# Moving the copies and the short transform of the middle column in a Fourier mixing and feed-forward kernel

## The chip, the cores and the metric

The kernel runs on one core of a Trainium2 chip. The metric is the device time of one execution in microseconds (us). The kernel before took 1976.9 us as the median of three runs (1976.07 to 1977.3). The profiled execution took 1976.83 us, of which 1975.0 us lie between its first and last instruction (the span).

## The reference

The input x has 8 batches of 3008 rows and 256 columns. Each batch is transformed along both axes and the real part kept; then every row goes through a feed-forward layer with the activation h cos(h).

```python
X = np.fft.fft(x, axis=1)
X = np.fft.fft(X, axis=2)
x = X.real.astype(np.float32).reshape(B * S, D)      # 24064 x 256
h = x @ w_in                                         # 256 -> 2048
g = h * np.cos(h)
out = g @ w_out                                      # 2048 -> 256
```

All types are float32.

## The kernel before

**The transform.** The 3008 rows are split as 47 x 64. A first half transforms over the 47 (`first_half`, eight chunks of a batch, two chunks for each quarter of x), its result goes to DRAM (`store_z`) and comes back in another layout (`load_z`), and a second half transforms over the 64 (`second_half`, six groups). The transform over the 256 columns is folded into the weights of the feed-forward layer. Since x is real, columns d and 256 - d are folded into their sum and difference (`fold`). Column 128 has no partner; it is called the middle column here. It is taken by itself: `take_middle` (L287) copies column 128 of one quarter of x, 94 x 8 numbers, on ScalarE into `xm`; `middle` (L291) clears 64 x 32 numbers of a PSUM bank on VectorE, adds two short matmul calls (four records in the profile) and copies the sum to `zm` on ScalarE. `keep_z` (L276), which takes each chunk out of PSUM, copies four columns of `zm` into it.

**The loop.** The feed-forward layer of a batch runs in 48 steps (six groups of columns by eight pieces of the 2048), 384 steps in all. The loop at L832 goes by half steps: `k` counts them, `t` is the step and `u` its half (0 even, 1 odd). While batch b goes through its 48 steps, batch b + 1 is transformed piece by piece: `transform` (L376) puts its calls into a list by step, and they are issued at the end of the odd half of that step (L909). For a quarter p of x, the load stands in step 2p, its copy of the middle column in step 2p + 2, the folds in steps 8p + 6 to 8p + 10, and a pair of first-half chunks in the even half of step 8p + 12. `middle` stands in step 10. "Step 10 of batch 1" below is the step 10 during which batch 1 is in the feed-forward layer and batch 2 is transformed. In batch 7 nothing is left to transform. Batch 0 follows an opening, in which batch 0 is transformed and the weights are loaded and folded; some of this is spread over steps 0 to 22 of batch 0 (`opening`, L797: sums of `w2` on POOL, and second halves in steps 5, 10, 14, 18 and 22).

**A half step.** The program writes every engine's instructions in an order fixed by hand, and each engine runs its own in that order. For half k (called cur; prev is k - 1, old is k - 2) the order is: `mm1(cur, 0)` on PE (L514) and `act_e` on ACT (L526, writes `ew`); in the even half of a step with a pair, the first chunk; `dve_g(old)` on DVE (L556) and, in every other half, `sums` on POOL (L572 to L579); the second chunk of a pair; `mm2` on PE (L605, three matmul calls of an older step); `act_round(prev)` on ACT (L542); the seed of half k + 1 on ACT (L495, which writes PSUM for the next `mm1`); `dve_frac(prev)` on DVE (L546); `act_sin(prev)` on ACT (L552); `mm1(cur, 1)` on PE; in some halves one more call of `mm2`; and `dve_h(cur)` on DVE (L530).

**Banks.** Four PSUM banks are handed out in turn to the halves (`psum` with tag H). `borrow(name, k)` takes the bank whose turn comes after k more, without taking the turn; its last user must be through with it.

**Transfers.** SP issues all of the loads and nearly all of the stores, in the order of the program. In the table of DMA traffic the opening fills the DMA engines for its first 70 us.

Of the kernel before, what the change touches and what calls it, by code (L numbers as in the profile page):

```python
# [22 lines left out]
NI = 32  # L23
# [85 lines left out]
def kernel(  # L109
# [7 lines left out]
    nc = tc.nc  # L117
# [85 lines left out]
    def psum(name, tag="H"):  # L203
        at = tag
        if tag == "H":
            at = f"H{turn[0] % 4}"
            turn[0] += 1
        return ppool.tile([128, 512], FP, tag=at, bufs=bank[tag], name=name)

    def borrow(name, k=0):  # L210
        return ppool.tile([128, 512], FP, tag=f"H{(turn[0] + k) % 4}", bufs=1, name=name)
# [28 lines left out]
    def first_half(b, c, pz=None):  # L240

        rows = 2 * N2 if b else 128
        fv = xfs.pop((b, c)).rearrange("r (e c) -> r e c", e=2)[0:rows]
        LE, LO, LE0, LO0 = (L[0:rows, 64 * q : 64 * q + 64] for q in range(4))
        pz = pz or psum("pz", "M")
        a = 128 if c == 0 else 0
        for e, (w, w0) in enumerate(((LE, LE0), (LO, LO0))):
            rows = slice(64 * e, 64 * e + 64)
            if a:
                nc.tensor.matmul(  # L250
                    pz[rows, 0:128], lhsT=w0, rhs=fv[:, e, 0:128], start=True, stop=True
                )
            nc.tensor.matmul(  # L253
                pz[rows, a:512],
                lhsT=w,
                rhs=fv[:, e, a:512],
                start=not a,
                stop=True,
                skip_group_check=True,
            )  # L260
        if b:
            return pz
        if a:
            nc.tensor.matmul(
                pz[64:128, 0:1], lhsT=LE0, rhs=fv[:, 1, 0:1], start=True, stop=True
            )
        nc.tensor.matmul(
            pz[64:128, a:512:128],
            lhsT=LE,
            rhs=fv[:, 1, a:512:128],  # L270
            start=True,
            stop=True,
        )
        keep_z(b, c, pz)

    def keep_z(b, c, pz):  # L276
        tag, n = ("zs", 4) if b or c < 4 else ("pq", 8)
        zs = spool.tile([128, 512], FP, tag=tag, bufs=n, name="zs")
        nc.scalar.copy(out=zs, in_=pz)
        if b:  # L280
            nc.scalar.copy(out=zs[64:128, 0:512:128], in_=zm[64:128, IP * c : IP * c + IP])
        zss[b, c] = zs

    xm = cpool.tile([128, NI], FP, tag="xm", name="xm")
    zm = cpool.tile([128, NI], FP, tag="zm", name="zm")
# [2 lines left out]
        xv = xs[b, p].rearrange("r (i d) -> r i d", d=ND)[0 : 2 * N2]  # L288
        nc.scalar.copy(out=xm[0 : 2 * N2, XP * p : XP * p + XP], in_=xv[:, :, 128])

    def middle(b):  # L291
        pm = borrow("pm")[64:128, 0:NI]
        nc.vector.memset(pm, 0.0)
        for i0, i1, q in ((0, 1, 2), (1, NI, 0)):
            nc.tensor.matmul(
                pm[:, i0:i1],
                lhsT=L[0 : 2 * N2, 64 * q : 64 * q + 64],
                rhs=xm[0 : 2 * N2, i0:i1],
                start=False,
                stop=True,  # L300
                skip_group_check=True,
            )
        nc.scalar.copy(out=zm[64:128], in_=pm)

    zds = {}
    z2s = {}
# [64 lines left out]
        nc.scalar.copy(out=nb[:, 0:T], in_=pn[:, 0:T])  # L371

    pairs = {}
    per = NG * 8

    def transform(b):  # L376
        todo = {}

        def at(o, *call):
            todo.setdefault(o, []).append(call)  # L380

        for p in range(4):
            at(2 * p, load_x, b, p)
            at(2 * p + 2, take_middle, b, p)
            for k in range(4):
                at(8 * p + (6, 7, 9, 10)[k], fold, b, 2 * p + k // 2, k % 2)
            pairs[per * (b - 1) + 8 * p + 12] = b, 2 * p
            for c in (2 * p, 2 * p + 1):
                at(8 * p + 12, store_z, b, c)
        at(10, middle, b)  # L390
        at(23, load_z, b, 0)
        at(39, load_z, b, 1)
        for g in range(NG):
            at(42 + g, second_half, b, g)
        return todo
# [138 lines left out]
    def sides(h):  # L534
        T = h.s.T
        return h.s.r[:, 2 * T * h.u : 2 * T * h.u + 2 * T], h.H[:, 0 : 2 * T]

    def act_round(h):
        if h.u == 0:
            h.s.r = spool.tile([128, 1024], FP, tag="r", bufs=4, name="r")  # L540
        r, y = sides(h)
        nc.scalar.activation(out=r, in_=y, func=AF.Copy, bias=BIG, scale=1.0)  # L542
# [41 lines left out]
    def mm2(s, lo, hi, order=range(7)):  # L584
        T = s.T
        key = (s.b, s.grp)
        if s.fp == 0 and lo == 0:
            acc[key] = []
            started[key] = set()
        gv, sv = blocks(s)  # L590
        todo = (
            (0, wv[:, 0, 0, s.fp], gv[:, 0, 0]),
            (1, wv[:, 1, 0, s.fp], gv[:, 1, 0]),
            (2, vx[:, 3, s.fp], gv[:, 1, 1]),
            (3, vx[:, 1, s.fp], sv[:, 0]),
            (4, vx[:, 0, s.fp], sv[:, 1]),
            (5, vx[:, 2, s.fp], sv[:, 2]),
            (6, wv[:, 1, 1, s.fp], sv[:, 3]),
        )
        for m, w, a in (todo[i] for i in order[lo:hi]):  # L600
            first = m // 2 not in started[key]
            if first:
                acc[key].append(psum("M", "M"))
            started[key].add(m // 2)
            nc.tensor.matmul(  # L605
                acc[key][m // 2][:, 256 * (m % 2) : 256 * (m % 2) + T],
                lhsT=w,
                rhs=a,
                start=first,
                stop=s.fp == 7,  # L610
                skip_group_check=True,
            )
# [210 lines left out]
    def unit(k):  # L823
        return halves[k] if 0 <= k < 2 * n else None
# [7 lines left out]
    for k in range(2 * n + LAG):  # L832
        t, u = divmod(k, 2)
        d, v = divmod(k - LAG, 2)
        cur, prev, old, nxt = unit(k), unit(k - 1), unit(k - 2), unit(k + 1)
        done = step(d)
        full = step(d if v else d - 1, True)
        if cur:
            if k % (2 * per) == 0:
                todo = transform(cur.s.b + 1) if cur.s.b + 1 < NB else {}  # L840
            if k not in range(3, AHEAD):
                mm1(cur, 0)
                if t == 0:
                    seed_first(cur)
                act_e(cur)
            if k == 0:
                spread_nb()
                fold_weights(1, 3)
            elif k == 1:
                pw = weights(0, 3)  # L850
            elif k == 2:
                pw = weight_row(3)
        pair = None if u else pairs.pop(t, None)
        if pair:
            b, c = pair
            pz = [first_half(b, c, borrow("pz"))]
        if old:
            dve_g(old)
            if old.u:
                sums(old.s)  # L860
        if pair:
            pz.append(first_half(b, c + 1, borrow("pz", 1)))
        if done:
            order = (0, 1, 5, 4, 3, 2, 6) if done is steps[-1] else range(7)
            mm2(done, 4 * v, 4 * v + 3, order)
        if full and full is not steps[-1]:
            take_m(full, 1 if v else 3, nc.vector)
        if nxt and 0 < k < AHEAD - 1:
            seed(nxt)
        if prev:  # L870
            act_round(prev)
        if pair:
            keep_z(b, c, pz[0])
        if nxt and k >= AHEAD - 1:
            seed(nxt)
        if full and full is not steps[-1]:
            take_m(full, 0 if v else 2, nc.scalar)
        if prev:
            dve_frac(prev)
        if k + 1 in range(3, AHEAD):  # L880
            mm1(nxt, 0)
            act_e(nxt)
        if prev:
            act_sin(prev)
        if pair:
            keep_z(b, c + 1, pz[1])
        if k == 1:
            keep_weights(0, 3, pw)
        elif k == 2:
            keep_wn(3, pw)  # L890
        if cur:
            mm1(cur, 1)
        if done and v == 0:
            mm2(done, 3, 4, order)
        if cur:
            dve_h(cur)
        if u == 0:
            continue
        for i in range(6):
            s = step(t - 4 - i, True)  # L900
            if s:
                combine_m(s, i)
        for sg, lag in ((0, 8), (1, 10)):
            s = step(t - lag, True)
            if s:
                store_out(s, sg)
        for call in opening.pop(t, ()):
            call[0](*call[1:])
        for call in todo.pop(t % per, ()):  # L909
            call[0](*call[1:])  # L910
# [31 lines left out]
```

## Time and profile before

| | |
|---|---|
| median of three runs | 1976.9 us |
| profiled execution | 1976.83 us |
| its span | 1975.0 us |
| busy: PE, ACT, DVE, POOL | 98%, 77%, 74%, 71% |
| granted TensorE clock, mean | 0.995 |

The span begins with the first instruction. PE is the matmul queue and PEld its weight loads; a row of the order of time has the start, the length, the engine, the line, what is written and read, and in brackets how long the engine stood idle before it and what ended that.

The length of a step can be read from the order of time: `act_e` (ACT, L526) runs once for each half, so the start of every second L526 marks a step, and the difference of two of them is a step's length. Some of these lengths, in us:

| step | batch 0 | batch 1 | batch 2 | batch 3 | batch 4 | batch 5 | batch 6 | batch 7 |
|---|---|---|---|---|---|---|---|---|
| 2 | 15.97 | 4.94 | 5.86 | 4.89 | 5.40 | 5.28 | 4.69 | 4.60 |
| 3 | 6.81 | 4.14 | 4.14 | 4.14 | 4.14 | 4.14 | 4.14 | 4.14 |
| 4 | 4.19 | 4.19 | 4.19 | 4.18 | 4.19 | 4.19 | 4.19 | 4.19 |
| 5 | 5.18 | 4.19 | 4.19 | 4.19 | 4.19 | 4.19 | 4.19 | 4.19 |
| 7 | 4.24 | 4.24 | 4.24 | 4.24 | 4.24 | 4.24 | 4.24 | 4.24 |
| 8 | 4.39 | 4.39 | 4.39 | 4.39 | 4.39 | 4.39 | 4.39 | 4.39 |
| 9 | 4.42 | 4.42 | 4.42 | 4.41 | 4.41 | 4.41 | 4.41 | 4.41 |
| 10 | 7.03 | 5.93 | 5.93 | 5.93 | 5.93 | 5.92 | 5.93 | 4.85 |
| 11 | 4.69 | 4.75 | 4.75 | 4.75 | 4.75 | 4.75 | 4.75 | 4.60 |
| 12 | 6.82 | 6.82 | 6.83 | 6.83 | 6.82 | 6.83 | 6.83 | 4.75 |
| 14 | 5.69 | 4.75 | 4.75 | 4.75 | 4.75 | 4.75 | 4.75 | 4.75 |
| 18 | 5.79 | 5.00 | 4.99 | 5.00 | 5.00 | 4.99 | 5.00 | 4.90 |
| 20 | 6.81 | 6.81 | 6.81 | 6.81 | 6.81 | 6.81 | 6.81 | 4.75 |

Steps 12 and 20 of batches 0 to 6 have a pair of first-half chunks. Groups of 225 columns go over into groups of 256 during steps 8 to 10.

### The profile page before, as it was taken

Reading aid. Unit: us, or ns where it says so; the run is one execution under the profiler, and the core shown is the slowest. Engines: PE = TensorE matmul, PEld = TensorE weight load, DVE = VectorE, ACT = ScalarE, POOL = GpSimd, SP = SyncE. Lnnn points to the kernel's source line nnn. Section 1 sums busy time; section 2 is a strip of 40 time slices with the busy share of each in tenths; the row PEclk is TensorE's granted clock in tenths of the full one; section 3 lists DMA queues with packets and bytes.
Section 4 is the critical chain, followed back from the end, with each engine's and each line's share of the span. In section 5 each row is a group of like instructions: output and inputs, shape, how many; then the busy total and the mean of one; then the engine's idle time right before and its main releaser. Section 6 shows DMA issues by size and latency. Waiting matters only on the chain.

```text
span 1975.0 us, 29718 instructions
## 1 busy us (share of the span) xinstructions
PE 1944.0 (98%) x9262; PEld 1688.1 (85%) x9262; DVE 1455.9 (74%) x2529; ACT 1519.6 (77%) x3450; POOL 1398.4 (71%) x1593
## 2 busy tenths in 40 slices
PE   9799999999999999999999999999999999999998
PEld 4788889888988889888888888988889888898887
DVE  3577778777777777777777777777777777778786
ACT  3577778777777777877878777777877787778775
POOL 3577767777677775778667876677766777666775
PEclk9899999999999999999999999999999999999999
DMA  8512014020241112301132022411114111100001
GB/s 200 118 25 46 22 41 85 22 42 19 46 82 26 36 26 59 71 18 40 40 60 51 20 41 41 84 23 38 26 41 85 24 40 28 38 22 16 12 15 29
DMA packets 176690, 88.70 MB, mean 45 GB/s; under 512 B 103303, under 2 KB 173622, under 8 KB 174902
## 3 DMA queue, kind: packets, MB, share of 16 engines
q1 hardware_dynamic: 176374, 86.68, 21.4%
q8 instruction: 75, 1.23, 0.3%
q14 instruction: 81, 0.66, 0.1%
q10 hardware_dynamic: 160, 0.13, 0.0%
HBM read 49.50 MB, written 37.27 MB: 44 GB/s over the span
## 4 chain that ended last, share of the span: by engine, by line
PE 89%; DMA 4%; DVE 3%; ACT 2%; SPq 1%; issue 0%; POOL 0%; DVEq 0%; ACTq 0%; POOLq 0%
PE M L605 53%; PE H L514 31%; PE pz L253 3%; DMA xp<-in_x_dram 2%; PE pb L339 2%; DVE r L546 1%; DMA zd<-zs 1%; ACT r L552 1%; DVE r L556 1%; ACT r L542 1%; DMA w<-in_moe_w_out_dram 0%; ACT ew L526 0%; DVE mr L630 0%; DMA wr<-in_moe_w_in_dram 0%; DMA out_dram<-ob 0%
## 5 line engine op out<-in xcount | busy, mean ns | idle before, releaser
L572 POOL TENSOR_TENSOR S<-r 128x512 f32<-128x512 f32 (+1 forms) x383 | 475.5, 1242 | 470.4 <-DVE r L556 423.5
L546 DVE SCALAR_TENSOR_TENSOR r<-r,H 128x512 f32<-128x512 f32 (+1 forms) x768 | 518.5, 675 | 222.3 <-ACT r L542 197.6
L552 ACT ACTIVATE r<-r 128x512 f32<-128x512 f32 (+1 forms) x768 | 477.5, 622 | 258.8 <-DVE r L546 256.2
L605 PE MATMUL M<-S,VX 128*128 128x256 f32 (+1 forms) x2304 | 615.7, 376 | 0.0
L556 DVE SCALAR_TENSOR_TENSOR r<-H,r 128x512 f32<-128x512 f32 (+1 forms) x768 | 518.8, 676 | 129.6 <-ACT r L552 86.6
L605 PEld LDWEIGHTS M<-S,VX 128*128 128x128 f32 x2304 | 435.9, 190 | 71.5 <-issue 22.7
L514 PE MATMUL H<-pq,WS 128*128 128x256 f32 (+1 forms) x1536 | 451.7, 376 | 11.9 <-ACT ew L526 11.9
L514 PE MATMUL H<-pq,WC 128*128 128x256 f32 (+1 forms) x1536 | 456.0, 379 | 2.8 <-ACT H L495 2.1
L542 ACT ACTIVATE r<-H 128x512 f32<-128x512 f32 (+1 forms) x768 | 447.5, 583 | 0.0
L530 DVE TENSOR_TENSOR H<-ew,H 128x256 f32<-128x256 f32 (+1 forms) x768 | 324.6, 423 | 139.7 <-PE H L514 79.3
L605 PE MATMUL M<-r,w 128*128 128x256 f32 (+1 forms) x1536 | 388.6, 375 | 0.0
L526 ACT ACTIVATE ew<-H 128x256 f32<-128x256 f32 (+1 forms) x768 | 288.3, 375 | 103.4 <-PE H L514 97.9
L495 ACT ACTIVATE H<-nb,wn 128x256 f32<-128x256 f32 (+1 forms) x766 | 365.6, 477 | 1.4
L514 PEld LDWEIGHTS H<-pq,WS 128*128 128x128 f32 x1536 | 290.9, 190 | 46.5 <-ACT ew L526 14.1
L605 PEld LDWEIGHTS M<-r,w 128*128 128x128 f32 x1536 | 300.5, 197 | 27.9 <-ACT mr L628 1.0
L514 PEld LDWEIGHTS H<-pq,WC 128*128 128x128 f32 x1536 | 280.0, 190 | 47.4 <-ACT H L495 15.1
L578 POOL TENSOR_TENSOR S<-S,r 128x256 f32<-128x256 f32 (+1 forms) x383 | 276.0, 721 | 30.0
L579 POOL TENSOR_TENSOR S<-r,S 128x256 f32<-128x256 f32 (+1 forms) x383 | 275.0, 718 | 30.0
L605 PE MATMUL M<-r,VX 128*128 128x256 f32 (+1 forms) x768 | 225.6, 375 | 0.0
L605 PE MATMUL M<-S,w 128*128 128x256 f32 (+1 forms) x768 | 225.2, 375 | 0.0
L605 PEld LDWEIGHTS M<-S,w 128*128 128x128 f32 x768 | 150.5, 196 | 14.6
L605 PEld LDWEIGHTS M<-r,VX 128*128 128x128 f32 x768 | 146.1, 190 | 14.7
(74 smaller groups left out, 927.4 us busy)
## 6 DMA issues: line engine op xcount, KB each, us to landing
out_dram<-ob SPq DMA_DIRECT2D x728, 32.0 KB
xp<-in_x_dram SPq DMA_DIRECT2D x56, 256.0 KB
zd<-zs SPq DMA_DIRECT2D x112, 96.0 KB
z<-zd SPq DMA_DIRECT2D x28, 384.0 KB
xp<-in_x_dram SPq DMA_DIRECT2D x56, 120.0 KB
nb<-nd SPq DMA_DIRECT2D x40, 128.0 KB
wr<-in_moe_w_in_dram SPq DMA_DIRECT2D x8, 256.0 KB
w<-in_moe_w_out_dram SPq DMA_DIRECT2D x4, 512.0 KB
```

The costliest lines, as they stand in the source:

```text
L495: nc.scalar.activation(out=h.H[:, 0:T], in_=s.nb[:, 0:T], func=AF.Copy, bias=0.25, scale=wn[:, f : f + 1])
L514: nc.tensor.matmul(h.H[:, 0:T], lhsT=W[:, 128 * f : 128 * f + 128], rhs=s.pq[:, e * T : e * T + T], start=False, stop=True, skip_group_che ...
L526: nc.scalar.mul(out=h.ew[:, 0:T], in_=h.H[:, 0:T], mul=2.0)
L530: nc.vector.tensor_tensor(out=h.H[:, T : 2 * T][:, ::-1], in0=h.ew[:, 0:T], in1=h.H[:, 0:T], op=ALU.subtract)
L542: nc.scalar.activation(out=r, in_=y, func=AF.Copy, bias=BIG, scale=1.0)
L546: nc.vector.scalar_tensor_tensor(out=r, in0=r, scalar=-BIG, in1=y, op0=ALU.add, op1=ALU.subtract)
L552: nc.scalar.activation(out=r, in_=r, func=AF.Sin, bias=0.0, scale=SIN_SCALE)
L556: nc.vector.scalar_tensor_tensor(out=r, in0=y, scalar=-0.25, in1=r, op0=ALU.add, op1=ALU.mult)
L572: tt(out=sv[:, 0:2], in0=qv[:, 1:2].to_broadcast([128, 2, T]), in1=qv[:, 0:4:3], op=ALU.subtract,)
L578: tt(out=sv[:, 2], in0=sv[:, 1], in1=gv[:, 0, 0], op=ALU.subtract)
L579: tt(out=sv[:, 3], in0=gv[:, 1, 0], in1=sv[:, 2], op=ALU.add)
L605: nc.tensor.matmul(acc[key][m // 2][:, 256 * (m % 2) : 256 * (m % 2) + T], lhsT=w, rhs=a, start=first, stop=s.fp == 7, skip_group_check=True,)
```

## The change

The copies of `take_middle` move from steps 2, 4, 6 and 8 to steps 7, 8, 9 and 10. `middle` leaves the list of step 10. It becomes two functions, called in the odd half of step 11: `clear_middle` borrows the bank after next and clears it on VectorE, behind `dve_g(old)` and ahead of `dve_frac`; `middle` issues the two matmul calls behind the first three calls of `mm2`. The copy to `zm` goes behind `act_round(prev)` and ahead of the seed on ScalarE. The instructions are the same as before in number and size.

```diff
@@ -288,9 +288,12 @@
-    def middle(b):
-        pm = borrow("pm")[64:128, 0:NI]
+    def clear_middle():
+        pm = borrow("pm", 1)[64:128, 0:NI]
         nc.vector.memset(pm, 0.0)
+        return pm
+
+    def middle(pm):
         for i0, i1, q in ((0, 1, 2), (1, NI, 0)):
             nc.tensor.matmul(
                 pm[:, i0:i1],
@@ -300,7 +303,6 @@
-        nc.scalar.copy(out=zm[64:128], in_=pm)
@@ -371,6 +373,7 @@
     pairs = {}
+    middles = set()
     per = NG * 8
@@ -381,13 +384,13 @@
         for p in range(4):
             at(2 * p, load_x, b, p)
-            at(2 * p + 2, take_middle, b, p)
+            at(7 + p, take_middle, b, p)
...
-        at(10, middle, b)
+        middles.add(per * (b - 1) + 11)
@@ -860,15 +863,20 @@
         if pair:
             pz.append(first_half(b, c + 1, borrow("pz", 1)))
+        pm = clear_middle() if u and t in middles else None
         if done:
             order = (0, 1, 5, 4, 3, 2, 6) if done is steps[-1] else range(7)
             mm2(done, 4 * v, 4 * v + 3, order)
+        if pm is not None:
+            middle(pm)
         if full and full is not steps[-1]:
             take_m(full, 1 if v else 3, nc.vector)
         if nxt and 0 < k < AHEAD - 1:
             seed(nxt)
         if prev:
             act_round(prev)
+        if pm is not None:
+            nc.scalar.copy(out=zm[64:128], in_=pm)
         if pair:
             keep_z(b, c, pz[0])
```

## The prediction

> **What bounds the kernel now.** I read the page first (busy shares), then the waits, the order of time around the copies and the middle call, the clock by window, and last the step lengths of the table above.
>
> From the page: TensorE's share, and the wait that the copies appear in.
>
> ```profile
> PE 1944.0 (98%) x9262; PEld 1688.1 (85%) x9262; DVE 1455.9 (74%) x2529; ACT 1519.6 (77%) x3450; POOL 1398.4 (71%) x1593
> ...
> L605 PE MATMUL M<-S,VX 128*128 128x256 f32 (+1 forms) x2304 | 615.7, 376 | 0.0
> ```
>
> The steady state is TensorE's: 98% busy, and the commonest matmul never waits. Only what makes TensorE idle or slow counts. The list of waits (who waits, for whom, total us, times, longest) has the candidates:
>
> ```profile
> ACT xm L289 <- DMA xp<-in_x_dram: 12.6, 3, 11.0
> ...
> PE H L514 <- ACT ew L526: 11.9, 4, 10.5
> ...
> PEld pm L295 <- DVE pm L293: 7.3, 7, 1.1
> ```
>
> One copy of `take_middle` waits 11.0 us for its columns of x, and one matmul waits 10.5 us for ScalarE. The order of time shows that they are one event, in step 2 of batch 0:
>
> ```profile
> 53.13 0.54 PE L514 MATMUL H<-pq,WC 128*128 128x225 f32 x2
> ...
> 53.27 0.58 ACT L552 ACTIVATE r<-r 128x450 f32<-128x450 f32 x1 [0.45 <-DVE r L546]
> ...
> 54.27 0.55 PE L605 MATMUL M<-S,w 128*128 128x225 f32 x2
> ...
> 64.83 0.20 ACT L289 COPY xm<-xp 94x8 f32<-94x8 f32 x1 [10.98 <-DMA xp<-in_x_dram]
> 64.94 0.35 ACT L526 ACTIVATE ew<-H 128x225 f32<-128x225 f32 x1
> ...
> 65.34 1.12 PE L514 MATMUL H<-pq,WS 128*128 128x225 f32 x2 [10.52 <-ACT ew L526]
> ```
>
> The `ew` of step 3 had its input from the matmul at 53.13 and stood behind the copy for 11 us. Then busy time by stretch (from, to, length, busy us of PE, PEld, DVE, ACT and POOL; the third number from the right is the granted clock, 1.00 at full speed, then the DMA engines' share and GB/s):
>
> ```profile
> 50.00:55.00 5.00, 4.46 (x22) 4.10 (x22) 3.74 (x7) 3.07 (x7) 3.11 (x5) 1.00 1.16 259
> 55.00:60.00 5.00, 0.00 (x0) 0.00 (x0) 0.00 (x0) 0.00 (x0) 0.33 (x1) 0.79 1.07 314
> ...
> 65.00:71.00 6.00, 5.66 (x15) 4.93 (x16) 3.00 (x6) 3.35 (x9) 3.12 (x5) 0.50 0.85 155
> 71.00:72.00 1.00, 1.00 (x5) 0.92 (x5) 0.19 (x1) 0.26 (x2) 0.65 (x1) 0.72 0.01 3
> ```
>
> TensorE comes out of the gap at half clock and stays there to about 71.56 (0.72 over the last microsecond). Last, the middle call in batch 1, order of time:
>
> ```profile
> 345.48 0.42 DVE L530 TENSOR_TENSOR H<-ew,H 128x256 f32<-128x256 f32 x1
> ...
> 345.98 0.09 DVE L293 MEMSET pm<- 64x32 f32 x1
> 346.12 0.31 PEld L295 LDWEIGHTS pm<-xm,L 94*64 94x64 f32 x4 [1.05 <-DVE pm L293]
> 346.12 0.42 PE L295 MATMUL pm<-xm,L 94*64 94x1 f32 x4 [0.65 <-DVE pm L293]
> ...
> 346.57 0.18 ACT L303 COPY zm<-pm 64x32 f32<-64x32 f32 x1 [0.25 <-PE pm L295]
> ```
>
> The clearing stands behind the `dve_h` of L530, so TensorE is 0.65 us without work.
>
> **Copies to steps 7 to 10, batch 0.** No DMA moves: the step issues only ScalarE copies, and SP's and POOL's queues keep their order. Without the copy, `ew` follows the sine at 53.85 (53.27 + 0.58), not at 64.94: 11.09 us. Step 3, run partly at half clock, took 6.81 us against 4.14 in batch 7: 2.67. Sum 13.76. TensorE's side agrees: 10.52 idle plus half of 6.22 us (65.34 to 71.56) is 13.63.
> The Trainium skill, page "TensorE: Matmul & The Clock Gate", Part 1, has the array back at full clock after one busy window of about 3.4 us, whose phase is free. This trace has 6.22 us at half clock, so the measurement decides; by one window (an estimate from that page) the loss would be 1.7 us in place of 2.67, and the result 1956.6.
>
> What is late next: the chain of waits has the third quarter of `w2` landing at 54.81 and `xp` of step 0 at 64.77.
>
> ```profile
> 46.47 8.34 DMA w<-in_moe_w_out_dram
> ...
> 54.83 9.94 DMA xp<-in_x_dram
> ```
>
> Steps 3 on would begin at 53.9, 58.0, 62.2, 67.4, 71.5. POOL asks for that piece of `w2` at the end of step 3 (58.0), the last piece let SP go on at 56.35 and is wanted at 67. POOL's fold of x and the first copy come at the ends of steps 6 and 7, at 71.5 and 75.8, some 7 to 11 us after x landed. Only the row of step 5's second half is close: `nd` goes out at 81.24 - 13.76 = 67.5 while the DMA engines are still full (to about 70); `nb` follows at 70.5 or sooner. The next `nb`, issued at 105.10, had its traffic done by 108 (the DMA share by stretch, another load among it): 2.9 us. That is 73.4, and the first seed of the next group wants it at 87.91 - 13.76 = 74.2. I take nothing; if it lands later, 0 to 6 us (bound: if it waited in the queue as long as x itself, 10 us, it would come at 80). Nothing more than the 13.76 can be gained here, as the steps that follow are already as long as in batch 7, where nothing is loaded.
>
> **Copies, batches 1 to 6.** Step 2 took 4.94, 5.86, 4.89, 5.40, 5.28, 4.69 us, 31.06 in all; in batch 7, with no copies, 4.60, or 27.60 in six. Gain 3.46. At the new places x landed four steps ago. Each copy is 0.19 us long, but where ScalarE has its input ready the next instruction starts 0.11 after it (64.83 to 64.94). Steps 4, 6 and 8 with copies are as long as in batch 7, and step 7 has the same room: nothing. Step 9's can hold a seed up by 0.11, which TensorE gets back in step 10, where it waits for ScalarE anyway: nothing, at worst 0.11. Step 10 has no room: in step 18 one small copy (L234) makes 5.00 of 4.90, 0.10. L234 and the moved copy both stand at the end of step 10: 0.21 together.
>
> **The middle call.** Steps 10 to 12 of batches 1 to 6 now take 5.93 + 4.75 + 6.82 = 17.50. Without the call: 4.85 + 4.60 from batch 7, step 20's 6.81 for a step with a pair, and 0.21 for the copies: 16.47. The new place, each queue in turn, with the times of batch 7's step 11:
> - DVE: `dve_g` ends at 1786.33, the clearing takes 0.09, so 1786.42 to 1786.49 with its signal. Behind it `dve_frac` slips 0.09, with `act_sin` after that, which the next line delays more.
> - PE: the first three matmul calls of `mm2` leave off at 1786.47. The middle's four records fill 0.42 (0.35 to the next start at 346.47). The wait of 0.65 is gone, 0.02 stays.
> - ACT: the copy to `zm` now waits in front of the seed. The round ends at 1786.37, the middle at about 1786.92, the copy at 1787.14, so the seed of the next half starts at 1787.05 (starts overlap by 0.1) instead of 1786.25: 0.8 late, ending 1787.53. Its matmul was due at 1787.34, with the middle ahead of it at 1787.76, its weight load 0.2 earlier: it loses about 0.05. The sine ends at 1788.08 and `ew` is due at 1788.39: no more loss.
> - The bank: the one that `pm` borrows is wanted next by the first chunk of the pair in step 12, behind the matmul at 1787.8; the copy at 1787.14 has freed it.
>
> So 16.47 + 0.42 + 0.05 = 16.94, a gain of 0.56 for each of six batches. Batch 0 took 7.03 + 4.69 + 6.82 = 18.54; 16.94 plus a second half (step 14: 5.69 - 4.75 = 0.94) is 17.88, gain 0.66. Together 4.0. Bounds: with ScalarE's copies hidden and 0.35 for the middle, 16.61, a gain of 0.89 each (6.2); with the whole 0.8 of the late seed passed on, 17.69, a loss of 0.19 (-1.3). I take the worked value, since the seed has slack by the same rows.
>
> **Sum.** 1976.83 (the profiled execution, 0.07 under the median of 1976.9) - 13.76 - 3.46 - 4.0 = 1955.6.
>
> **The rivals.**
> - Another wait takes over in the opening. For it: the DMA engines are full until 70, and `nb` has about 1 us in hand. Against: all else landed 3 us or more ahead. Landing at 80, 5.8 after the seed wants it, it costs 5.8: 1961.4. Chance 0.15.
> - ScalarE's new wait eats the middle's gain: the late seed passed on whole, 1.3 lost instead of 4.0 gained: 1960.9. For it: ScalarE is the limit in step 10. Against: the spare time worked out above. Chance 0.13.
> - The change does not do what it says: the copies wait again at their new place. Against: x landed at 64.8. Only the fourth part, sent out after step 6 (about 69) and taken at the end of step 10 (about 89), is later; it would have to take 20 us. With all of the 13.76 back: 1969.4. Chance 0.03.
> - Slower: the clock. Some 3.1 us after TensorE's last matmul (54.8) the clock fell (0.79 over 55 to 60 puts that at 57.9), and the half-speed stretch behind the gap cost 2.67 more. If steps 3 to 8 were fed in pieces by late transfers, each gap of 3.1 us would so cost 5.8; five of them 29: 1984.6. It decides from four (23.2 against 21.2 gained). For it: one such gap did it here. Against: no transfer due in these steps lands late. Chance 0.04.
>
> The Trainium skill, "TensorE: Matmul & The Clock Gate", Part 1, says that an idle window of about 3.4 us closes the gate again, so that a gap is paid twice; this trace has 3.1 us.
>
> **How the numbers follow.** The forecast has 0.65, with its own range 1953.4 (middle at its best) to 1958.5 (`nb` 3 us late). The range 1953.0 to 1962.5 takes in the first two rivals; the other two, 0.07, and part of the tails stay out. Within 0.2% is 4 us either way, about what a measurement can tell: faster 0.65 + 0.15 + 0.13 + 0.03, less 0.01 for a case between, is 0.95; same 0.01; slower 0.04.
>
> **What would show it.** In the profile after: no wait of ScalarE for x in the copies; step 2 of batch 0 some 4.9 us and step 3 some 4.1; a granted clock of 1.00 from 50 on; step 2 of batches 1 to 6 at 4.60; steps 10 to 12 near 16.9 with a wait of ScalarE's copy to `zm` of about 0.6 and none of TensorE for the clearing. Wrong would make it: a gap of TensorE between 54 and 75, or a seed wait in steps 11 and 12 above 0.3.

## The result

The changed kernel takes 1958.85 us as the median of four runs (1957.18 to 1959.07), 1976.99 before: a ratio of 0.9907, 95% interval 0.989 to 0.9924. On a second chip it was 1958.36 against 1979.01, 0.9898 (0.9883 to 0.9913). The profiled execution took 1957.18, its span is 1955.4 us, and the mean granted clock is 0.999.

From the page, the shares of the engines and the matmul group:

```profile
PE 1940.8 (99%) x9262; PEld 1686.2 (86%) x9262; DVE 1455.8 (74%) x2529; ACT 1516.3 (78%) x3450; POOL 1396.4 (71%) x1593
...
L608 PE MATMUL M<-S,VX 128*128 128x256 f32 (+1 forms) x2304 | 615.7, 376 | 0.0
```

TensorE does the same work in a span that is 19.6 us shorter. The list of waits (who waits, for whom, total us, times, longest), for 40 to 75 us and then for the whole span, answers to the lines shown of before:

```profile
PE H L517 <- ACT H L498: 2.1, 2, 1.1
...
ACT H L498 <- DMA nb<-nd: 1.3, 1, 1.3
```

```profile
ACT zm L879 <- PE pm L298: 4.6, 7, 0.7
...
PEld pm L298 <- DVE pm L293: 2.3, 7, 0.3
```

The copy to `zm` waited before, too, but for less:

```profile
ACT zm L303 <- PE pm L295: 2.1, 7, 0.6
```

No copy waits for x any more. One wait is new: a seed of the opening waits for `nb`. (A second half stores one row of its result to DRAM as `nd`, and `nb` is that row read back to all 128 partitions; the seeds of that group of columns need it.) One is longer: the copy to `zm` waits for the middle call 0.66 us in each of seven batches, 0.30 before. Busy time by stretch (from, to, length, busy us of PE, PEld, DVE, ACT, POOL, then the granted clock, DMA share and GB/s):

```profile
50.00:55.00 5.00, 5.00 (x27) 4.91 (x28) 4.13 (x9) 3.88 (x10) 3.06 (x4) 1.00 1.16 245
55.00:60.00 5.00, 5.00 (x28) 4.94 (x27) 3.94 (x8) 4.12 (x11) 3.77 (x5) 1.00 1.07 322
...
65.00:71.00 6.00, 6.00 (x37) 5.83 (x36) 3.82 (x9) 4.41 (x11) 4.85 (x7) 1.00 0.86 168
```

The gap is gone, and the clock stays at 1.00 in this execution. Step lengths by the starts of `act_e`, as in the table of before:

| | before | after | difference |
|---|---|---|---|
| start of step 0 | 38.96 | 38.52 | -0.44 |
| steps 0 to 3 of batch 0 | 32.78 | 18.93 | -13.85 |
| step 7 of batch 0 | 4.24 | 5.29 | +1.05 |
| step 2 of batches 1 to 6, sum | 31.05 | 27.57 | -3.48 |
| steps 10 to 12, batch 0 | 18.54 | 17.75 | -0.79 |
| steps 10 to 12, batches 1 to 6, each | 17.50 | 17.03 | -0.47 |
| other steps (0.2 to 0.4 in four of them) | | | +0.75 |

With six times 0.47 this adds up to 19.58 of the 19.63 by which the span fell. The four steps of the last line are 42 of batch 0 (+0.23), 34 of batch 3 and 26 of batch 6 (+0.37 each) and 42 of batch 6 (-0.21). They come in every profile below that has the call in step 11 and in none that has it in step 10; what causes them was not looked for further.

### The profile page after: what moved, and what is told of

It is laid out like the page before. It is cut to its first block, busy times and chain, and to the rows that moved or that the text cites. A ratio compares the mean times of both kernels' runs of the same rounds, so it can differ in the third digit from the quotient of the medians.

```text
span 1955.4 us, 29697 instructions
## 1 busy us (share of the span) xinstructions
PE 1940.8 (99%) x9262; PEld 1686.2 (86%) x9262; DVE 1455.8 (74%) x2529; ACT 1516.3 (78%) x3450; POOL 1396.4 (71%) x1593
## 4 chain that ended last, share of the span: by engine, by line
PE 97%; DMA 1%; ACT 0%; DVE 0%; SPq 0%; issue 0%; POOL 0%; POOLq 0%; ACTq 0%
PE M L608 58%; PE H L517 33%; PE pz L253 3%; PE pb L341 2%; DMA xp<-in_x_dram 1%; PE pw L408 0%; DMA wr<-in_moe_w_in_dram 0%; DMA nb<-nd 0%; DMA nd<-pq 0%; PE pz L250 0%; PE pm L298 0%; PE pd L464 0%; DVE r L549 0%; ACT H L498 0%; ACT r L555 0%
```

## The experiments

**The copies alone.**

```diff
 (kernel before)
-            at(2 * p + 2, take_middle, b, p)
+            at(7 + p, take_middle, b, p)
```

> The copies stand in steps 7 to 10, the middle call stays at the end of step 10 with its clearing behind dve_h. Theory (the copies carry the gain, through the opening): step 2 of batch 0 near 4.8 and step 3 near 4.15 as in the changed kernel (13.9 us), step 2 of batches 1 to 6 at 4.60 (3.5 us), step 7 of batch 0 about 1 us long over its 4.24 (the wait for nb), steps 10 to 12 at 17.5 as before; 1960 to 1962. Rival (the call carries it, and the copies' wait comes back elsewhere): 1970 or more.

Measured: 1963.14 (1961.79 to 1964.34) against 1977.82 before on this chip, a ratio of 0.9929 (0.9915 to 0.9944). Steps 0 to 3 of batch 0 take 18.93, step 2 of the six batches 27.57 in all, step 7 of batch 0 is 5.42. Steps 10 to 12 of batches 1 to 6 are 17.75, a quarter of a microsecond longer than before: the fourth copy now stands ahead of the call at the end of step 10, and the weights of the call's second half wait for it, so that its four records fill 0.67 us instead of 0.42:

```profile
333.12 0.19 PEld L295 LDWEIGHTS pm<-xm,L 94*64 94x64 f32 x2 [0.17 <-ACT xm L289]
```

The copies carry the gain.

**The call alone.**

```diff
 (changed kernel)
-            at(7 + p, take_middle, b, p)
+            at(2 * p + 2, take_middle, b, p)
```

> The call in the odd half of step 11, the copies left in steps 2 to 8. Theory: step 2 of batch 0 stays at 16.0 and step 3 at 6.8; steps 10 to 12 of batches 1 to 6 go from 17.50 to about 16.9, a little under the 17.03 of the changed kernel, since step 10 has one ScalarE copy less; 1972.5 to 1973. Rival (ScalarE's wait in front of the seed eats it): 17.5 or more, 1976.5 to 1978.

Measured: 1973.52 (ten runs), 0.9981 (0.9972 to 0.999). Steps 10 to 12 take 16.92 in each of the six batches and 17.64 in batch 0. Step 2 of batch 0 took 17.53 and step 3 5.31 in the profile; their sum is that of before (22.84 against 22.78), but by another road: x landed later, at 66.7, and the half clock behind the gap was shorter.

```profile
67.27 1.12 PE L517 MATMUL H<-pq,WS 128*128 128x225 f32 x2 [12.08 <-ACT ew L529]
```

```profile
60.00:61.00 1.00, 0.00 (x0) 0.00 (x0) 0.00 (x0) 0.00 (x0) 0.00 (x0) 0.60 1.01 132
...
70.00:71.00 1.00, 1.00 (x5) 0.91 (x5) 0.62 (x1) 0.65 (x2) 0.92 (x2) 0.78 1.17 144
```

By these rows TensorE stopped at 55.2, the clock fell at 60.2, 5.0 us later, and half clock lasted for 3.2 us of work (67.3 to 70.4), where the kernel before had 6.2. The call itself can be read from steps 10 to 12 alone: its new place is worth 0.6 a batch, and the copy to `zm` ahead of the seed does not eat it. The two parts, 14.7 and 4.3 us, add up to 19.0; the whole change gave 18.1 and 20.7 on the two chips.

**The copies of batch 1 alone** (those that run in batch 0's steps).

```diff
 (kernel before)
-            at(2 * p + 2, take_middle, b, p)
+            at(7 + p if b == 1 else 2 * p + 2, take_middle, b, p)
```

> The kernel before with the four copies of batch 1 alone in steps 7 to 10 (those that run in batch 0's steps); the other batches and the call as before. Theory: the opening alone is worth 13.9 less about 1.1 for nb, so 1964 to 1966. Rival (the waits of batches 1 to 6 and the call carry most): 1970 or more.

Measured: 1964.89 (1964.24 to 1966.67), 0.994 (0.9925 to 0.9955). Most of the gain of the copies (12.9 of 14.7 us) is in the opening. This profile also showed what none had so far: no gap, and yet the clock was at half from 49.1 to 55.9, and step 2 of batch 0 took 7.34 instead of 4.78.

**One copy alone.**

```diff
 (kernel before)
-            at(2 * p + 2, take_middle, b, p)
+            at(7 if b == 1 and p == 0 else 2 * p + 2, take_middle, b, p)
```

> The kernel before with one copy moved: the first quarter of batch 1, from step 2 to step 7. Theory (the DMA queue is what ScalarE meets, whichever copy stands first): the wait goes to the copy at the end of step 4, at 62, whose quarter lands at 66 to 67: a wait of some 4.5 us, TensorE idle for about 3.9 of it and, if the clock falls after some 3 us, half speed for some us: 1967 to 1970.5. Rival (only that one copy's transfer is late): 1964 to 1966, as with all four moved.

Measured: 1972.64 (nine runs, 1969.97 to 1975.25), 0.9978 (0.9968 to 0.9988). The waits of its stretch from 55 to 80 us, and busy time and clock by stretch:

```profile
ACT xm L289 <- DMA xp<-in_x_dram: 6.0, 1, 6.0
...
PE H L514 <- ACT ew L526: 5.4, 1, 5.4
```

```profile
60.00:65.00 5.00, 4.70 (x25) 4.29 (x23) 3.20 (x6) 2.83 (x7) 4.53 (x7) 1.00 1.10 187
65.00:70.00 5.00, 0.00 (x0) 0.00 (x0) 0.00 (x0) 0.43 (x3) 1.24 (x2) 0.76 1.00 187
70.00:75.00 5.00, 4.92 (x15) 4.30 (x16) 2.49 (x5) 3.08 (x8) 1.98 (x3) 0.56 0.14 24
```

The wait went to the next copy, the one at the end of step 4, and was longer than I had worked out (6.0 for 4.5). The clock fell again: TensorE stopped at 64.7, and 0.76 over the next stretch puts the fall at 67.6, 2.9 us later. This profile has half clock without a gap as well, from 50.5 to 53.9, and its step 2 of batch 0 took 6.42 instead of 4.78. Of the 12.9 us that moving all four gained, 5.2 are left. ScalarE meets the queue, whether the first copy or the second stands ahead.

**The half clock behind the gap, by itself.** The copies stay where they were; TensorE gets work that nobody uses while it waits.

```diff
 (kernel before)
+        if k == 6:
+            pd = borrow("pd")
+            for i in range(22):
+                nc.tensor.matmul(
+                    pd[:, 0:256], lhsT=CS[0][:, 0:128], rhs=CS[0], start=True, stop=True
+                )
         if cur:
             mm1(cur, 1)
```

> The kernel before, with the copies where they were, and 22 matmul calls of 256 columns (used by nobody, 0.43 each, 9.4 in all) in front of the second matmul of half step 6, where TensorE stands idle for 10.5. Theory (the half clock behind the gap is a cost of its own): step 2 of batch 0 stays at about 16 to 17.5, step 3 goes from 6.8 to about 4.2; 2.6 under the kernel before (a ratio of 0.9987), less in runs that had their own spell. Rival (step 3 is long because the other engines start late): step 3 stays at 6 or more, no change in all.

Measured: 1976.21 (eleven runs) against 1977.86, 0.9992 (0.9983 to 1.0). Step 2 is 16.37 and step 3 4.14, 2.67 under the 6.81 of before. By stretch:

```profile
55.00:60.00 5.00, 5.00 (x25) 4.53 (x24) 0.34 (x1) 0.00 (x0) 0.70 (x2) 1.00 1.08 341
60.00:65.00 5.00, 5.00 (x25) 4.40 (x24) 0.00 (x0) 0.00 (x0) 0.00 (x0) 1.00 1.08 199
65.00:71.00 6.00, 5.88 (x30) 5.10 (x29) 3.85 (x8) 4.63 (x13) 2.75 (x4) 1.00 0.82 163
```

The wait of ScalarE is as long as before (10.7), but the clock stays at 1.00. So 2.67 of the 13.8 us in the opening are the clock's in the profile of before, and keeping the waiting TensorE busy gets them back in step 3; as step 2 is 0.4 longer here, steps 0 to 3 are 2.3 us shorter. The span is not shorter (1975.4): steps 2 and 3 of batch 2 took 2.4 us more. There the clock fell to half from 551.7 to 555.2, shortly after a wait of TensorE of 1.5 us:

```profile
550.45 0.65 PE L514 MATMUL H<-pq,WS 128*128 128x225 f32 x2 [1.54 <-ACT ew L526]
```

```profile
552.00:553.00 1.00, 1.00 (x4) 0.89 (x3) 0.81 (x2) 1.00 (x4) 0.10 (x1) 0.50 0.91 245
```

In the median the filling gained 1.6, and the interval just reaches no change. That is less than 2.67, and the other profiles with a gap say why it may be: the step behind it was 1.2 to 1.9 us over its usual length in them (step 3 was 5.31 with the call alone and 6.06 in a profile below, for 4.14; step 5 was 6.85 for 5.18 with one copy alone).

**The changed kernel again, and the loads behind `nb`.** The kernel's own runs had a spread with two candidates: the half clock that the third experiment showed, and the landing of `nb`. The first of these runs is the changed kernel as it is, the second puts two loads later.

```diff
 (changed kernel)
-            at(2 * p, load_x, b, p)
+            at(4 + p if b == 1 and p > 1 else 2 * p, load_x, b, p)
```

> The changed kernel once more, on one chip with the next three. Its profiled execution took 1957.2 at a mean clock of 0.999, its other runs 1958.8 to 1959.1 at 0.997. Theory A (a spell of half clock, which falls in most runs between 49 and 56, where TensorE is busy only about half of the time from 46.5 to 50.5): runs either near 1957 to 1958 without a spell or 1.5 to 3 longer with one. Theory B (the later landing of nb makes the spread): the same times with step 7 of batch 0 between 5 and 8 long.

> The changed kernel with the loads of the third and fourth quarter of batch 1's x put behind step 5's nd and nb (steps 6 and 7 in place of 4 and 6). Theory: nb lands about 71 and the wait of 1.3 goes: step 7 of batch 0 goes from 5.3 to 4.24 in the profile, 1.0 less in all. Theory A leaves the spread of the runs as it is; theory B takes it away, and the median falls by 2.5 to 3. If nb was not late for the queue, nothing changes.

Measured: the changed kernel 1958.36 (1957.43 to 1958.93), step 7 of batch 0 at 5.70, no half clock in the profile. With the loads behind: 1958.66 (1958.18 to 1959.53), a ratio to before of 0.99 (0.9884 to 0.9917), no shorter. Yet step 7 is 4.24 in its profile. The order of time shows `nd` and `nb` in the changed kernel and then with the loads behind:

```profile
66.94 0.22 SPq L364 DMA_DIRECT2D nd<-pq  x1
...
70.78 0.36 SPq L365 DMA_DIRECT2D nb<-nd  x1
...
74.99 0.48 ACT L498 ACTIVATE H<-nb,wn 128x256 f32<-128x256 f32 x1 [1.28 <-DMA nb<-nd]
...
75.52 0.70 PE L517 MATMUL H<-pq,WC 128*128 128x256 f32 x2 [0.78 <-ACT H L498]
```

```profile
69.98 0.22 SPq L364 DMA_DIRECT2D nd<-pq  x1
...
71.07 0.35 SPq L365 DMA_DIRECT2D nb<-nd  x1
...
76.64 0.48 ACT L498 ACTIVATE H<-nb,wn 128x256 f32<-128x256 f32 x1
```

`nd`, one row, took 3.8 us behind the loads of x, and 1.1 without them; the seed no longer waits. Here `nd` also went out 3 us later, when the DMA engines had run empty; the kernel with three edits below settles that, as it has the same order of loads and no half clock: out at 67.58, `nd` took 1.1 there too. What the loads' new place gained, the clock took. By stretch, with the loads behind:

```profile
46.00:48.00 2.00, 1.28 (x7) 0.90 (x6) 1.06 (x3) 1.67 (x6) 0.51 (x1) 1.00 1.20 205
48.00:49.00 1.00, 0.61 (x2) 0.58 (x3) 0.76 (x2) 0.80 (x2) 0.33 (x1) 0.74 1.24 177
49.00:51.00 2.00, 1.50 (x5) 0.84 (x4) 1.21 (x3) 1.50 (x4) 1.84 (x3) 0.50 1.23 191
51.00:55.00 4.00, 4.00 (x12) 3.57 (x12) 2.34 (x5) 2.51 (x6) 1.52 (x3) 0.50 1.15 248
55.00:56.00 1.00, 1.00 (x6) 0.99 (x5) 0.46 (x2) 0.00 (x0) 0.92 (x2) 0.85 1.20 391
```

Half clock from about 48.5 to 55.3. Steps 0 to 3 of batch 0 take 21.42 here, 18.93 in the changed kernel's two profiles: this spell of half clock costs 2.5 us. It comes out of steps 1 and 2, where TensorE waits 1.1 and 1.0 us for seeds and was busy for about half of the time. All four of these runs have a clock of 0.997 or 0.998, three of the changed kernel's first four 0.997. The half clock and the wait for `nb` hide each other: where the spell makes the opening later, `nb` is in time (step 7 is 4.24 with the loads in their old place in the third experiment).

**The opening filled.**

```diff
 (changed kernel)
+        if k in (2, 3):
+            pd = psum("pd", "M")
+            for i in range(2):
+                nc.tensor.matmul(
+                    pd[:, 0:256], lhsT=CS[0][:, 0:128], rhs=CS[0], start=True, stop=True
+                )
         if cur:
             dve_h(cur)
```

> The changed kernel with two matmul calls of 256 columns, used by nobody, behind the second matmul of each of half steps 2 and 3, where TensorE waits 1.1 and 1.0 for the seeds. They fit into these waits (about 0.9 each). Theory A: the granted clock is 1.00 from 40 to 60 in every run, the profile stays at about 1957 and the median falls to it, 1.5 to 2 less than the changed kernel's. Theory B: median and spread as the changed kernel's. If the filling is in the way of the seeds' matmuls: up to 1 longer.

Measured: 1958.72 (1956.16 to 1960.72), 0.99 (0.9885 to 0.9915). Clock 0.998 to 0.999 in all runs, 1.00 from 36 to 90 in the profile, and still a spread of 4.5 us. So the clock alone does not make the spread. Step 7 was 4.81 in the profiled run, the shortest; that `nb` is what made the others longer was not seen in a profile.

**The same filling in the kernel before.** The edit is the one above, on the kernel before.

> The kernel before with the filling of half steps 2 and 3 (two matmul calls of 256 columns behind each). Theory: in the kernel before the end of step 2 is set by the landing of x at 65, so a spell of half clock before it costs nothing, and its absence gains nothing: the times of the kernel before within 0.5 (a ratio of 0.9995 to 1.0005). Rival (the spell costs the kernel before as much as the changed one): 1.5 to 2.5 less.

Measured: 1978.03 (eleven runs) against 1977.86, 1.0002 (0.9993 to 1.0011). In the kernel before no gain is seen; the interval leaves room for 1.4 us. The copy waits 13.3 us in this profile:

```profile
ACT xm L289 <- DMA xp<-in_x_dram: 13.3, 1, 13.3
```

ScalarE came to the copy at 53.6, as before (53.9), since the profile of before has no spell that filling could take away; x landed 2 us later (66.9 for 64.8). That a spell in the kernel before would be covered by this wait is shown by the profile with TensorE kept busy: it had half clock from 50.0 to 53.4, ahead of the wait, and ScalarE still waited 10.7 us for x.

**Three edits together, without and with the filling.** The loads behind `nb`, the copies one step earlier, and the copy to `zm` behind the sine:

```diff
 (changed kernel)
-            at(2 * p, load_x, b, p)
-            at(7 + p, take_middle, b, p)
+            at(4 + p if b == 1 and p > 1 else 2 * p, load_x, b, p)
+            at(6 + p, take_middle, b, p)
...
-        if pm is not None:
-            nc.scalar.copy(out=zm[64:128], in_=pm)
...
         if prev:
             act_sin(prev)
+        if pm is not None:
+            nc.scalar.copy(out=zm[64:128], in_=pm)
```

> The changed kernel with three things: the loads behind nb as in the run above, the copies of the middle column one step earlier (6 to 9, so that step 10 has one ScalarE copy less) and the copy to zm behind the sine instead of ahead of the seed. Theory: step 7 of batch 0 at 4.24 (1.0), step 10 at 4.95 instead of 5.06 (0.11 in each of seven batches), steps 11 and 12 at 11.92 instead of 11.97 (0.05 in each): 2.1 under the changed kernel, about 1955 in the profile. Rival (ScalarE's wait for zm or the copies do not bound TensorE): 1.0 from the loads alone.

> The three edits of e8 and the filling of half steps 2 and 3 together. Theory (the changed kernel's spread has two sources, the spell and the wait for nb, and the two add): granted clock 0.999 in every run, step 7 of batch 0 at 4.24, all runs within about 1 of 1956, the median at 1955.5 to 1956.5. Rival (a third source, as the runs with the filling alone went from 1956.2 to 1960.7 at 0.999): runs over 1957.5 at 0.999 remain.

Measured without the filling: 1956.45 (1955.93 to 1958.28), 0.9891 (0.9876 to 0.9905). Step 7 of batch 0 is 4.24, step 10 of the later batches 4.95, steps 10 to 12 16.92. Step 11 is 5.14, as with the copy to `zm` ahead of the seed: that wait cost nothing. Three runs have a clock of 0.999 and take 1955.9 to 1956.8, the one at 0.997 takes 1958.3. With the filling: 1955.98 (1955.21 to 1956.17), 0.989 (0.9876 to 0.9903), all four runs at 0.999 and within 1 us. The medians of the two are not told apart from the changed kernel's by their intervals; by the spans of the profiles (1954.1 and 1954.4 against 1955.4 and 1956.4) they are 1.0 to 2.3 us shorter.

**The call one place later.**

```diff
 (the kernel above with the filling)
-        if pm is not None:
-            middle(pm)
...
         if cur:
             mm1(cur, 1)
+        if pm is not None:
+            middle(pm)
```

> As e11, with the middle call's two matmul calls one place later in step 11, behind the second matmul of the half (mm1 with e = 1) instead of ahead of it. In the changed kernel TensorE stands 0.09 between mm2 and the call, for the signal of the clearing. Theory: that goes, step 11 from 5.15 to about 5.06, steps 10 to 12 to 16.83, 0.6 under e11 in all. Rival (the matmuls behind, or the copy to zm, which comes later, take it back): 5.15 or more.

Measured: 1955.71 (1954.97 to 1957.2), 0.989 (0.9875 to 0.9905). With both sources of the spread taken away, here and in the run above, seven of eight runs lie between 1955.0 and 1956.2; the eighth, 1957.2 at a clock of 0.999, has something else, which stays open. Step 11 stays at 5.14 and steps 10 to 12 at 16.92. Order of time in step 11 of batch 1, first with the call in its place (the three edits) and then one place later:

```profile
334.20 0.59 PE L608 MATMUL M<-r,VX 128*128 128x256 f32 x2
...
334.72 0.31 PEld L298 LDWEIGHTS pm<-xm,L 94*64 94x64 f32 x4 [0.33 <-DVE pm L293]
334.73 0.42 PE L298 MATMUL pm<-xm,L 94*64 94x1 f32 x4
...
335.07 0.70 PE L517 MATMUL H<-pq,WS 128*128 128x256 f32 x2
335.39 0.41 PEld L608 LDWEIGHTS M<-S,VX 128*128 128x128 f32 x2
335.61 0.59 PE L608 MATMUL M<-S,VX 128*128 128x256 f32 x2
```

```profile
334.26 0.59 PE L517 MATMUL H<-pq,WS 128*128 128x256 f32 x2
334.79 0.31 PEld L298 LDWEIGHTS pm<-xm,L 94*64 94x64 f32 x4 [0.33 <-issue]
334.79 0.42 PE L298 MATMUL pm<-xm,L 94*64 94x1 f32 x4
...
335.14 0.70 PE L608 MATMUL M<-S,VX 128*128 128x256 f32 x2
335.46 0.41 PEld L517 LDWEIGHTS H<-pq,WC 128*128 128x128 f32 x2
335.67 0.59 PE L517 MATMUL H<-pq,WC 128*128 128x256 f32 x2
```

One place later the clearing is long done, and the call starts 0.53 us after the matmul ahead of it (334.26 to 334.79), as it does in its old place (334.20 to 334.73); matmuls without a call between them follow after 0.43. So the 0.10 is not the signal of the clearing, and my theory of this run falls. The call costs 0.10 ahead of it, 0.34 itself, and 0.11 on the matmul behind (0.54 to the next instead of 0.43): 0.55 in both places. Its weight loads, 137 ns each by the summary of the tile, come to 0.55 for four; that they set the price was not tested.

## Why the prediction was right, and where it was off

- *Copies, batch 0: 13.76.* Measured 13.85 in the profile, and the third experiment has most of it by itself. Of this 2.67 were put down to the clock; with TensorE kept busy step 3 was shorter by that. The mechanism is right, but the agreement to 0.1 is luck of the profile that was read: steps 0 to 3 with the copies in their old place took 32.78, 32.85 and 34.33 us in three profiles, as x landed between 64.8 and 66.9, and half clock behind the gap lasted 6.2, 3.2 and 4.7 us. The loss of 2.67 is the greatest of the four profiles with a gap; the 1.7 that the prediction works out beside it and sets aside is nearer to the other three (1.2, 1.7 and 1.9).
- *Nothing for what is late next, with `nb` the one close case.* The mechanism of the first rival came, in a smaller size: 1.05 and 1.47 in the two profiles of the changed kernel, for the 5.8 of its worst case. The step that failed is "`nb` follows at 70.5 or sooner ... 2.9 us": it followed at 70.78 and took 4.2, and ScalarE was ready for the seed at 73.7 instead of 74.2. The chain of waits of the changed kernel has both:

```profile
66.94 3.83 DMA nd<-pq
...
70.78 4.19 DMA nb<-nd
```

Why `nb` itself took 4.2 where 2.9 was taken stays open: the DMA engines were busy for only 0.10 of the time from 71 to 72, so the loads ahead of it were through; the last loads of x were issued behind it, from 71.2 on.

- *Copies, batches 1 to 6: 3.46.* Measured 3.48.
- *The call: 4.0.* Measured 0.79 + 6 x 0.47 = 3.6. The term that was mis-sized is the call on TensorE, 0.42 and 0.05 for a late seed: it is 0.55, and the late seed costs nothing, as the copy to `zm` behind the sine showed. The copies at the end of step 10 came out as worked out: 5.06 against 4.85.
- *Slower by the clock.* That rival did not come: no gap. But the forecast had no term for a clock that falls without one. The kernel before has the same thin stretch at 46.5 to 50.5, ahead of the wait for x, which covers a spell there. With the wait gone the spell is in the open: 2.5 us by the profile with the loads behind `nb`, less the 1.05 of `nb` that it hides. Three of the changed kernel's first runs are 1.6 to 1.9 longer than its profiled one, at a lower clock. That the spell is what they have is argued from this and from the runs with both sources removed; no profile of the changed kernel itself shows it.
- The sum of 1955.6 stands to the profiled 1957.18 by: 1.05 for `nb`, 0.4 for the call, 0.75 for four steps whose change is not explained, less 0.44 of an earlier start and 0.1 for the opening. The median is 3.25 over the forecast, within the range.

## What to carry to other kernels

A copy that nobody needs yet, put early on an engine that works in program order, makes everything behind it wait for the transfer; place it by when its consumer wants it, and move every copy of the kind, since the next one meets the same queue. When a long wait goes, look for what it covered: here a stretch of half clock and a late row of one kilobyte, each worth 1 to 2.5 us and each hiding the other. A difference of this size is read from step lengths of several profiles rather than from one median.

## What the runs showed of the hardware

- The clock falls without a long gap. From 46.5 to 50.5 TensorE was busy for about half of the time, with idle pieces of 1.1 us and less; in four of ten profiles in which this stretch was not filled the clock fell to half between 48.5 and 50.5, for 3.4 to 6.8 us, and in none of the four in which it was filled. In one profile the clock also fell in batch 2, after a single idle piece of 1.5 us.
- The Trainium skill, "TensorE: Matmul & The Clock Gate", Part 1, has windows of 3.4 us of free phase. The traces agree on the phase: the fall comes at another time in each profile, or not at all; in an empty gap it came 2.9, 3.1, 3.8 and 5.0 us after the last matmul, and half clock lasted 3.2, 4.3, 4.7 and 6.2 us of work behind it. Two of the falls came sooner than a whole window; that windows which are only half empty suffice is argued from these runs.
- A DMA of one kilobyte behind loads that filled the DMA engines took 3.8 us, and 1.1 with the loads put behind it.
- A call of four records with 64 columns of weights and at most 31 columns of data held TensorE for 0.55 us, where its rows show 0.42.
